# Replanning an instruction order: transfers at traced length, spare time for buffers, outputs and routing

## The chip, the cores and the metric

The kernel runs on one core of a Trainium2 chip. The metric is the device time of one execution in microseconds; the median of three executions is what is compared. The profile shows one execution in detail.

## The reference: what is computed

Three parts follow each other. A linear recurrence runs over 768 time steps for 4 x 8 heads, with a 40 x 40 state per head:

```
y[t]  = r[t] @ state
Sa    = state @ a[t]
state = state * w[t] - outer(Sa, b[t]) + outer(v[t], k[t])
```

Its output, 3072 tokens of 320 numbers, is routed: each token goes to the one of 8 experts with the largest gate logit, through a two-layer net with ReLU (320 to 1024 to 320), and is scaled by its gate probability. A last dense two-layer net (320 to 2048 to 320, leaky ReLU) follows for all tokens. Everything is in float32.

## The kernel before

The recurrence is done in chunks of 32 time steps. The 768 time steps are 6 blocks (`i`) of 4 chunks (`g`), and the heads come in two halves (`hf`), so that there are 48 steps `s = 8 i + 2 g + hf`. For each block and half (`n = 2 i + hf`) the inputs are loaded in two parts (`load(n, h)`: tiles `w`, `KB`, `AE`), decay products are formed on DVE and POOL (`prep`: L371 to L381), and inner products of the chunks on PE (`gram`: L409), which go to DRAM (`Md`). For a whole block they come back as `Mu`, a triangular system is solved in 14 rounds on DVE (`inverse`: L450, L452), the result goes to DRAM (`Td`, `Tad`) and back as `TB` and `Rt` (`back`), and `fix` completes it (PE L476, L485). Then for each step: `rv(s)` loads `RE` and `MV`, `kbt` transposes (L512), `chain` carries the state (PE L542, L553, L570, DVE L574), `output` forms the result (PE L590, L603, L622, DVE L611). After every fourth step of a half, `Router.add` computes the gate and scatters rows to `xs` with an indirect transfer from POOL (L870). Eight transfers `xs<-maskZ` of 563.5 KB (`zero_region`, L809) fill the regions of the experts beforehand. The two nets follow, with an order written out by hand, in which nothing is planned.

The order of all the work of the recurrence is made when the kernel is built, by a list scheduler, `Sched`. Each `op` has an engine (`V` DVE, `A` ACT, `P` POOL, `T` PE, `S` SyncE), a duration, tiles read and written, and for a transfer a length `xfer`. `run` computes for each operation a level (how early it must start so that what follows meets its due time, which `when(s)` sets to `START + STEP * s`) and then places the operations one after the other: on each engine among those that could start soonest, that with the highest level. `PATIENCE`, `SLACK` and `ALPHA` weigh the level against starting later. On the planned time line transfers share one bus, and at most eight are under way (`lanes`). Where PE's planned gap is over `GAP`, the plan fills a share of it (`FILL` 0.8, in the startup `FILL0` 0.685) with matmuls that compute nothing that is used (L724); they keep TensorE active. What comes out is only an order for each engine: at run time every engine goes through its list in that order, and each instruction waits for its data. The planned times do not bind.

All loads, the round trips over DRAM and the zero regions are issued by SyncE (SP) in one list, so a transfer whose buffer is still in use holds back all that stand behind it.

Of the kernel before, what the change touches and what calls it, by code (L numbers as in the profile page):

```python
# [26 lines left out]
class Sched:  # L27
# [7 lines left out]
    def __init__(self, eng):  # L35
        self.eng = dict(zip('VAPTS', eng))
        self.ops = []
        self.due = 1e9
        self.since = 0.
        self.slack = 0.  # L40
        self.w, self.r = {}, {}

    def op(self, on, dur, fn, r=(), w=(), ring=None, done=0., grp=None, xfer=0., banks=(), sel=False, act=None):

        i = len(self.ops)
        deps = set()
        for k in r:
            if k in self.w:
                deps.add(self.w[k])
        for k in w:  # L50
            if k in self.w:
                deps.add(self.w[k])
            deps.update(self.r.get(k, ()))
        deps.discard(i)
        for k in r:
            self.r.setdefault(k, set()).add(i)
        for k in w:
            self.w[k] = i
            self.r[k] = set()
        on = on if isinstance(on, dict) else {on: dur}  # L60
        self.ops.append(dict(on=on, fn=fn, deps=deps, ring=ring, done=done, grp=grp, users=0, ps=None, xfer=xfer, banks=list(banks), due=self.due, since=self.since, slack=self.slack, sel=sel, act=act))
        return i

    def psum(self, i, j):
# [18 lines left out]
    def run(self):  # L83
        ops = self.ops
        n = len(ops)
        succ = [[] for _ in ops]
        for i, o in enumerate(ops):
            for d in o['deps']:
                succ[d].append(i)
        lag = lambda o, e: self.AFTER[e] + o['done'] + (o['xfer'] + 1.5 if o['xfer'] else 0.)  # L90
        level = [0.] * n
        for i in range(n - 1, -1, -1):
            o = ops[i]
            e, d = min(o['on'].items(), key=lambda x: x[1])
            level[i] = d + max([level[j] + lag(o, e) for j in succ[i]] + [-o['due']])
        left = [len(o['deps']) for o in ops]
        at = [o['since'] for o in ops]
        free = {e: 0. for e in 'VAPTS'}
# [7 lines left out]
        grp = {}  # L106
# [13 lines left out]
        while placed < n:  # L120
            best = None
            for e in 'VAPTS':
                cand = []
                for i in wait[e]:
                    o = ops[i]
# [82 lines left out]
            seen = end + self.AFTER[e] + o['done']  # L208
            if o['xfer']:
                bus = max(bus, end + .65) + o['xfer']  # L210
                seen = bus + .95
                lanes = lanes[1:] + [seen]
            if o['done'] > 1.:
                scat = max(scat, seen)
            for j in succ[i]:
                left[j] -= 1
                at[j] = max(at[j], seen)
                if not left[j]:
                    offer(j)
        self.end = max(free.values())  # L220
# [8 lines left out]

    TICK, LEAST, COLD, FILL1 = 10.24 / 3, 3060., 1.85, 12.  # L230
    GAP, FILL, FILL0, FILLT = 0.24, 0.8, 0.685, 60.0
    SLACK, PATIENCE, ALPHA = 0.075, 30.677, 0.105


NV, QI, GS = 1, 'S', 0
SLACK0, LD0, LDS, PR0, PRS, LATEW, RV0, ZR0, ZRS, GR = 0.268, 0.0, 3.0, 15.245, 0, 0, 40.584, 52.618, 7.65, 1
NMV, NRE, NNI, NZ, NWT = 6, 7, 2, 3, 6


START, STEP = 66.553, 7.916  # L240
DPREP, DINV, DOUT, DTURN, DFIX = (-1.52, -1.13, -0.18, 1.52), (2.13, 2.32), 1.968, 0.886, 6.599
EVT = 'A'
EZ = 'AV'
PM, ZM = 0, 0
# [29 lines left out]
def attention(ctx, tc, I, R, eng):  # L274
# [62 lines left out]
    def masks(E):  # L337
# [2 lines left out]
            P.affine_select(maskP[o:o + 32], maskP[o:o + 32], [[1, 32]], ALU.is_gt, 0.0, base=0, channel_multiplier=-1)  # L340
        P.memset(maskZ, 0.0)
        P.iota(maskZ.bitcast(I32)[:, D:D + 1], [[0, 1]], base=NT, channel_multiplier=0)
    def dma(o, i, nb, r, w, on='S'):
        op(on, .48 if on == 'S' else .06, lambda E: E.dma_start(o, i), r, w, xfer=max(.18, nb / 360e3))  # L344

    def hold(i, fn):
        pass
# [1 line left out]
    def load(n, h):  # L349
        i, hf = divmod(n, 2)  # L350
        a = n % 4
        late = ['Mu'] if n in (2, 3) else []
        dma(ws[hf][:, h, 0:528], I['wT'][hf, i, :, 528 * h:528 * h + 528], 270336, late if LATEW else (), [('w', hf, h)])
        dma(KBs[a][:, 2 * h:2 * h + 2].rearrange("x g p a t -> x (g p a t)"), I['kbT'][hf, i, :, 1024 * h:1024 * h + 1024], 1 << 19, late, [('KB', a, h)])
        src = I['aT'][hf, i].rearrange("x (j g c) -> x j g c", j=2, g=4)[:, :, 2 * h:2 * h + 2]
        zero = [('AEs', a, j, g, par) for j in range(2) for g in (2 * h, 2 * h + 1) for par in range(2)]
        if i:
            dma(AEs[a][:, :, 2 * h:2 * h + 2].rearrange("x j g p t -> x j (g p t)"), src.rearrange("x j g c -> x j (g c)"), 1 << 19, late, [('AEo', a, j, h) for j in range(2)] + zero)
        else:
            for j in range(2):  # L360
                o, r = SIG[j], RHO[j]
                op('P', .45, lambda E, o=o, j=j: E.memset(AEs[a][o:o + 64, j, 2 * h:2 * h + 2], 0.0), (), zero[4 * j:4 * j + 4])
                dma(AEs[a][r:r + 64, j, 2 * h:2 * h + 2].rearrange("x g p t -> x (g p t)"), src[r:r + 64, j].rearrange("x g c -> x (g c)"), 1 << 17, late, [('AEo', a, j, h)])
# [71 lines left out]
    def when(s):  # L435
        Q.due = START + STEP * s
# [20 lines left out]
    def back(i):  # L457

        for gp in range(2):
            dma(TB4s[i % 2][:, gp].rearrange("s h u t -> s (h u) t"), Tds[i % 2][16 * gp:16 * gp + 16].rearrange("u q s t -> (q s) u t"), 262144,  # L460
                [('Td', i % 2)], [('TB', 4 * (i % 2) + 2 * gp + h) for h in range(2)], QI)
        for q in range(4):
            dma(R4[32 * q:32 * q + 16].rearrange("s m u t -> s (m u) t"), Tads[i % 2][:, q].rearrange("u s t -> s u t"), 80000, [('Tad', i % 2)], [('Rt', m, q) for m in range(4)], QI)
# [31 lines left out]
    def rv(s):  # L495
        i, g, hf, n = info(s)
        RE, MV = REs[s % NRE], MVs[s % NMV]
        dma(RE.rearrange("x j p t -> x (j p t)"), I['rT'][hf, i, :, 512 * g:512 * g + 512], 1 << 18, (), [('REo', s % NRE, j) for j in range(2)] + [('REs', s % NRE, j, par) for j in range(2) for par in range(2)])
        for j in range(2):
            r, o = RHO[j], SIG[j]  # L500
            dma(MV[o:o + 32, :, MC[j]], I['vt'][hf, i, j, :, 320 * g:320 * g + 320].rearrange("x (p e) -> x p e", e=40), 40960 * 4, (), [('MVv', s % NMV, j)])
            if s < 2:
                op('P', .35, lambda E, r=r, j=j: E.memset(MV[r:r + 40, :, MC[j]], 0.0), (), [('MVs', s % NMV, j)])

# [77 lines left out]
    def output(s):  # L582
# [41 lines left out]
        if g == 3:  # L624
            xk = []
            for bb in range(2):
                x = (2 * n + bb) % R.NXB
                xk.append(x)
                u = 8 * bb
                while u < 8 * bb + 8:  # L630
                    b, col = place(hf, u)
                    m = min(8 * bb + 8 - u, 12 - col // 40)
                    op('V', .15 + .0416 * m, lambda E, x=x, u=u, b=b, col=col, m=m, bb=bb:
                       E.tensor_tensor(R.xbs[x][:, 40 * (u - 8 * bb):40 * (u - 8 * bb) + 40 * m], py[:, b, col:col + 40 * m], Wts[n % NWT][:, u:u + m, :].rearrange("p h e -> p (h e)"), ALU.mult),
                       [('py', hf, k) for k in range(4)] + [('Wt', n % NWT, h, j) for h in range(2) for j in range(2)], [('xb', x, u)], banks=[('py', b)])
                    u += m
            R.add(Q, psum, copy, ev, hf, i, xk)


    Q.slack = SLACK0  # L640
# [48 lines left out]
    for i in range(6):  # L689
        if i < 5:  # L690
            for h in range(2):
                for n in (2 * i + 2, 2 * i + 3):
                    when(8 * i + DPREP[2 * h + n % 2])
                    load(n, h)
                    prep(n, h)
                    for g in (2 * h, 2 * h + 1):
                        gram(n, g)
            inverse(i + 1)
            when(8 * i + DFIX)
            back(i + 1)  # L700
            for x in range(4):
                when(8 * i + DFIX + .5 + x // 2 * 1.5)
                fix(i + 1, x % 2, x // 2)
            when(8 * i + DTURN)
            turn(2 * i + 2)
            turn(2 * i + 3)
        for c in range(8):
            s = 8 * i + c
            _, g, hf, n = info(s)
            when(s)  # L710
            Q.since = RV0 if 2 <= s < 8 else 0.
            rv(s)
            Q.since = 0.
            kbt(s)
            chain(s)
            if i == 0 and c < 4:
                Q.since = ZR0 + ZRS * c
                for e in (2 * c, 2 * c + 1):
                    R.zero_region(Q, e, maskZ, [('X', s % 2)])
                Q.since = 0.  # L720
            when(s + DOUT)
            output(s)
    Q.run()
    Q.emit(lambda: T.matmul(py[:, 2, 320:448], R.one, R.one, start=True, stop=True))  # L724
    R.finish(psum)
# [701 lines left out]
```

## Time and profile before

| what | value |
|---|---|
| time, median of 3 runs | 1150.17 us (1149.91 to 1153.44) |
| the profiled execution's own time | 1148.05 us |
| its span, first to last instruction | 1146.3 us |
| mean granted TensorE clock | 0.931 |
| PE busy | 1009.7 us, 88% |
| DVE, ACT, POOL busy | 735.6, 552.8, 378.5 us |
| time on the last chain: PE, DVE, issue, DMA, SP queue | 56%, 14%, 13%, 5%, 3% |

The first 545 us of the span are the recurrence with its routing, the rest are the two nets. A granted clock of 1.0 is 2.4 GHz and 0.5 is 1.2 GHz. "issue" is time in which an engine waited for nothing that the profile shows.

### The profile page before, as it was taken

What the parts mean: (1) busy time and instruction counts of PE and PEld (TensorE: products, weight loads), DVE (VectorE), ACT (ScalarE), POOL (GpSimd) and SP (SyncE); (2) the same over time, 40 slices, a digit from 0 to 9 for tenths busy, and PEclk for the clock granted to TensorE, in tenths of its full rate; (3) what the DMA queues carried; (4) which work ended last, traced back from release to release, by engine and by line L of the source; (5) the groups of instructions that cost most, each with busy time, mean ns of one, the idle gap of its engine ahead of it and who ended that gap; (6) DMA issues with size and microseconds to landing.
All of it is one profiled execution on the core that took longest, in us unless ns stands there. A gap on an engine that the chain in (4) does not pass through costs nothing.

```text
span 1146.3 us, 37065 instructions
## 1 busy us (share of the span) xinstructions
PE 1009.7 (88%) x15918; PEld 906.1 (79%) x15918; DVE 735.6 (64%) x1571; ACT 552.8 (48%) x1264; POOL 378.5 (33%) x318
## 2 busy tenths in 40 slices
PE   4677777888878879989589999999999999999997
PEld 4665667777767767778588888999989999999997
DVE  7984676976967856344577787786764444444453
ACT  4114554856746747667434434434533333333343
POOL 8232112222223221010155565662849191010100
PEclk9876888998989988889799999999999999999999
DMA  7659463653734723330565666753311010000000
GB/s 201 202 135 250 100 164 90 178 150 110 194 98 146 172 64 98 72 98 12 165 224 175 199 197 199 217 170 107 99 32 51 18 30 18 7 18 7 23 13 14
DMA packets 146123, 129.44 MB, mean 113 GB/s; under 512 B 102176, under 2 KB 110624, under 8 KB 145952
## 3 DMA queue, kind: packets, MB, share of 16 engines
q1 hardware_dynamic: 143648, 119.11, 37.7%
q0 software_dynamic: 2304, 7.89, 1.9%
q8 instruction: 127, 2.08, 0.8%
q14 instruction: 44, 0.36, 0.1%
HBM read 102.13 MB, written 24.85 MB: 111 GB/s over the span
## 4 chain that ended last, share of the span: by engine, by line
PE 56%; DVE 14%; issue 13%; ACT 6%; DMA 5%; POOL 3%; SPq 3%; POOLq 0%; DVEq 0%; ACTq 0%
PE ph L981 17%; PE py L622 4%; PE oy L1188 3%; PE oy L1187 3%; PE oy L1186 3%; PE ch L570 2%; PE tr L590 2%; SPq L344 2%; PE tr L409 2%; ACT Z L292 2%; PE tr L512 2%; DVE tmp L450 2%; ACT NI L292 2%; PE y L1046 2%; PE tr L485 2%
## 5 line engine op out<-in xcount | busy, mean ns | idle before, releaser
L981 PE MATMUL ph<-xt,wq 128*128 128x512 f32 (+2 forms) x1408 | 311.5, 364 | 5.0 <-DVE xt L1022 5.0
L981 PEld LDWEIGHTS ph<-xt,wq 128*128 128x128 f32 x1408 | 248.0, 189 | 35.5 <-DVE xt L1022 6.5
L1166 DVE TENSOR_TENSOR gf<-gf,ph 128x512 f32<-128x512 f32 (+1 forms) x112 | 68.4, 610 | 98.8 <-ACT gf L1165 98.4
L1170 DVE TENSOR_TENSOR gl<-gf,gh 128x512 fp32r<-128x512 f32 (+1 forms) x112 | 76.7, 684 | 70.1 <-ACT gh L1169 70.1
L1165 ACT ACTIVATE gf<-ph 128x512 f32<-128x512 f32 (+1 forms) x112 | 60.0, 536 | 109.5 <-PE ph L981 109.0
L292 ACT COPY Z<-tr 40x512 f32<-40x512 f32 x192 | 98.3, 540 | 22.9 <-PE tr L590 21.2
L1169 ACT CAST gh<-gf 128x512 fp32r<-128x512 f32 (+1 forms) x112 | 62.7, 559 | 96.3 <-DVE gf L1166 96.3
L381 POOL TENSOR_TENSOR KB<-KB,w 128x1024 f32<-128x1024 f32 x21 | 47.2, 2245 | 159.4 <-PE py L622 34.4
L1196 POOL DMA_INDIRECT out_dram<-ob,gid x24 | 23.9, 995 | 218.5 <-ACT ob L1195 213.3
L1032 ACT ACTIVATE gh<-ph 128x448 fp32r<-128x448 f32 x64 | 34.9, 546 | 120.3 <-PE ph L981 120.3
L1188 PE MATMUL oy<-wo,gl 128*128 128x320 f32 x288 | 89.2, 310 | 0.1
L1187 PE MATMUL oy<-wo,gh 128*128 128x320 f32 x288 | 88.9, 309 | 0.0
L1186 PE MATMUL oy<-wo,gh 128*128 128x320 f32 x288 | 88.8, 308 | 0.0
L622 PE MATMUL py<-Z,RE 128*32 128x40 f32 x1536 | 73.7, 212 | 6.1 <-DVE RE L611 4.6
L611 DVE TENSOR_TENSOR RE<-tr,maskP 64x128 f32<-64x128 f32 x192 | 55.1, 287 | 34.3 <-PE tr L603 30.4
L622 PEld LDWEIGHTS py<-Z,RE 128*32 128x32 f32 x1536 | 65.8, 120 | 13.6 <-DVE RE L611 7.5
L1046 PE MATMUL y<-gh,wo 128*128 128x448 f32 x192 | 73.1, 381 | 3.0 <-DVE Y L1053 2.8
L574 DVE TENSOR_TENSOR MV<-ch,WC 40x320 f32<-40x320 f32 x92 | 44.9, 488 | 45.3 <-PE ch L570 43.7
L870 POOL DMA_INDIRECT xs<-xb,rii x24 | 25.6, 1068 | 142.0 <-DVE rii L860 95.2
L1049 PE MATMUL y<-gl,wo 128*128 128x448 f32 x192 | 70.9, 369 | 0.0
L292 ACT COPY NI<-tr 64x160 f32<-64x160 f32 x192 | 55.1, 287 | 23.3 <-PE tr L512 20.0
L590 PE MATMUL tr<-ident,MV 128*104 128x128 f32 x384 | 60.2, 290 | 5.1 <-ACT NI L292 4.1
(173 smaller groups left out, 2206.2 us busy)
## 6 DMA issues: line engine op xcount, KB each, us to landing
KB<-in_kbT_dram SPq DMA_DIRECT2D x24, 512.0 KB, 6.0
RE<-in_rT_dram SPq DMA_DIRECT2D x48, 256.0 KB, 4.3
AE<-in_aT_dram SPq DMA_DIRECT2D x20, 512.0 KB, 6.3
raw<-in_wo_dram SPq DMA_DIRECT2D x16, 640.0 KB, 5.2
raw<-in_wqa_dram SPq DMA_DIRECT2D x16, 512.0 KB, 4.1
w<-in_wT_dram SPq DMA_DIRECT2D x24, 264.0 KB, 4.6
xs<-maskZ SPq DMA_DIRECT2D x8, 563.5 KB, 5.5
win<-xs SPq DMA_DIRECT2D x8, 563.5 KB, 10.0
```

Source lines behind the costliest of these rows:

```text
L292: (E.copy if E is A else E.tensor_copy)(o, i)
L590: E.transpose(c['t'][0:104, q, :], MV[:, 4 * h + q], ident)
L622: E.matmul(py[32 * g:32 * g + 32, b, col:col + 40], RE[:, j, p, :], Z[:, p, ZC[j]:ZC[j] + 40], start=True, stop=True)
L981: T.matmul(ph, l, r, start=k == 0, stop=k == 7)
L1046: T.matmul(y[c], hi, gh, start=m == 0, stop=False)
L1049: T.matmul(y[c], hi, gl, start=False, stop=m == 7)
L1166: V.tensor_tensor(gf, gf, ph, ALU.max)
L1169: A.copy(gh, gf)
L1170: V.tensor_tensor(gl, gf, gh.bitcast(F32), ALU.subtract)
L1186: T.matmul(o, gh[:, sl], w[:, 0:320], start=m == 0, stop=False)
L1187: T.matmul(o, gh[:, sl], w[:, 320:640], start=False, stop=False)
L1188: T.matmul(o, gl[:, sl], w[:, 0:320], start=False, stop=m == 15)
```

## The change

Only constants and rules of the planner change; the instructions themselves, their tiles and buffers stay. A transfer is planned with a bus rate of 230e3 bytes per us instead of 360e3, with 2.0 us instead of 0.95 us from its end to being seen, and with a further 0.816 us (`LATE`) for whoever reads it. A load marked `free=True` (w, KB, AE, RE, MV) is placed on the planned line no sooner than 4.829 us (`SPARE`) after the last user of its buffer, and that user becomes more urgent by as much. Each dependency of an output's operations has 0.065 us (`SPO`) of spare time, of routing and `fix` 0.296 us (`SPF`). `load` is due 0.127 steps ahead of its `prep`. The due times and weights have new values.

```diff
-    def op(self, on, dur, fn, r=(), w=(), ring=None, done=0., grp=None, xfer=0., banks=(), sel=False, act=None):
+    def op(self, on, dur, fn, r=(), w=(), ring=None, done=0., grp=None, xfer=0., banks=(), sel=False, act=None, free=False):
...
-        self.ops.append(dict(on=on, fn=fn, deps=deps, ring=ring, done=done, grp=grp, users=0, ps=None, xfer=xfer, banks=list(banks), due=self.due, since=self.since, slack=self.slack, sel=sel, act=act))
+        self.ops.append(dict(on=on, fn=fn, deps=deps, ring=ring, done=done, grp=grp, users=0, ps=None, xfer=xfer, banks=list(banks), due=self.due, since=self.since, slack=self.slack, sel=sel, act=act, spare=self.spare if on.keys() != {'S'} else self.SPARE if xfer and free else 0.))
...
-        lag = lambda o, e: self.AFTER[e] + o['done'] + (o['xfer'] + 1.5 if o['xfer'] else 0.)
+        lag = lambda o, e: self.AFTER[e] + o['done'] + (o['xfer'] + 2.2 if o['xfer'] else 0.)
...
-            level[i] = d + max([level[j] + lag(o, e) for j in succ[i]] + [-o['due']])
+            level[i] = d + max([level[j] + lag(o, e) + ops[j]['spare'] for j in succ[i]] + [-o['due']])
...
-                seen = bus + .95
+                seen = bus + 2.
...
-                at[j] = max(at[j], seen)
+                at[j] = max(at[j], seen + ops[j]['spare'] + (self.LATE if o['xfer'] else 0.))
...
-    SLACK, PATIENCE, ALPHA = 0.075, 30.677, 0.105
+    SPARE, LATE = 4.829, 0.816
+    SLACK, PATIENCE, ALPHA = 0.075, 47.288, 0.091
...
-SLACK0, LD0, LDS, PR0, PRS, LATEW, RV0, ZR0, ZRS, GR = 0.268, 0.0, 3.0, 15.245, 0, 0, 40.584, 52.618, 7.65, 1
+SLACK0, LD0, LDS, PR0, PRS, LATEW, RV0, ZR0, ZRS, GR = 0.338, 0.0, 3.0, 14.472, 0.072, 0, 40.584, 52.618, 7.65, 1
...
-START, STEP = 66.553, 7.916
-DPREP, DINV, DOUT, DTURN, DFIX = (-1.52, -1.13, -0.18, 1.52), (2.13, 2.32), 1.968, 0.886, 6.599
+LEAD, SPO, SPF = 0.127, 0.065, 0.296
+START, STEP = 72.1, 8.135
+DPREP, DINV, DOUT, DTURN, DFIX = (-1.52, -1.13, -0.18, 1.52), (2.28, 3.1), 1.966, 1.269, 7.992
...
-    def dma(o, i, nb, r, w, on='S'):
-        op(on, .48 if on == 'S' else .06, lambda E: E.dma_start(o, i), r, w, xfer=max(.18, nb / 360e3))
+    def dma(o, i, nb, r, w, on='S', free=False):
+        op(on, .48 if on == 'S' else .06, lambda E: E.dma_start(o, i), r, w, xfer=max(.18, nb / 230e3), free=free)
...
-            dma(TB4s[i % 2][:, gp].rearrange("s h u t -> s (h u) t"), Tds[i % 2][16 * gp:16 * gp + 16].rearrange("u q s t -> (q s) u t"), 262144,
+            dma(TB4s[i % 2][:, gp].rearrange("s h u t -> s (h u) t"), Tds[i % 2][16 * gp:16 * gp + 16].rearrange("u q s t -> (q s) u t"), 400000,
...
+            Q.spare = SPF
             R.add(Q, psum, copy, ev, hf, i, xk)
+            Q.spare = SPO
...
+                    when(8 * i + DPREP[2 * h + n % 2] - LEAD)
+                    load(n, h)
                     when(8 * i + DPREP[2 * h + n % 2])
-                    load(n, h)
                     prep(n, h)
...
+                Q.spare = SPF
                 fix(i + 1, x % 2, x // 2)
+                Q.spare = 0.
...
             when(s + DOUT)
+            Q.spare = SPO
             output(s)
+            Q.spare = 0.
```

## Rows read from the trace of the kernel before

**Rows 1.** Windows by stage, all engines; columns in the first row.
```profile
core 0: us, PE busy (x) PEld busy (x) DVE busy (x) ACT busy (x) POOL busy (x), PEclk, DMA share, GB/s
0.00:66.00 66.00, 37.47 (x595) 34.93 (x595) 57.54 (x110) 19.41 (x43) 37.23 (x69) 0.90 0.62 180
66.00:92.00 26.00, 19.80 (x504) 17.99 (x506) 16.60 (x35) 5.85 (x19) 6.12 (x3) 0.71 0.73 169
92.00:124.00 32.00, 20.15 (x602) 16.92 (x601) 16.02 (x31) 14.17 (x41) 5.82 (x4) 0.71 0.87 232
124.00:187.00 63.00, 52.70 (x1640) 45.57 (x1637) 49.04 (x137) 35.25 (x99) 12.54 (x8) 0.86 0.50 124
187.00:504.00 317.00, 267.32 (x8338) 232.75 (x8338) 218.26 (x662) 204.46 (x574) 71.46 (x65) 0.89 0.47 122
504.00:545.00 41.00, 39.09 (x1066) 33.62 (x1064) 18.83 (x64) 32.30 (x87) 2.31 (x6) 1.00 0.21 59
545.00:1146.30 601.30, 573.19 (x3204) 524.35 (x3193) 359.28 (x537) 241.32 (x402) 243.02 (x165) 0.98 0.31 94
```

**Rows 2.** Waits of PE, 187 to 545: total us, times, longest.
```profile
PE tr L485 <- issue: 9.7, 6, 2.3
...
PE tr L590 <- ACT NI L292: 3.8, 5, 1.0
...
PE py L724 <- issue: 0.3, 1, 0.3
...
PE tr L590 <- ACT MV L292: 0.2, 1, 0.2
```

**Rows 3.** DMA queues and issues of the whole span: count, KB, us to landing.
```profile
q8 instruction: 127, 2.08, 0.8%
...
KB<-in_kbT_dram SPq DMA_DIRECT2D x24, 512.0 KB, 6.0
...
xs<-maskZ SPq DMA_DIRECT2D x8, 563.5 KB, 5.5
```

**Rows 4.** DMA view, whole span, same columns.
```profile
TB<-Td SPq DMA_DIRECT2D x12, 256.0 KB, 4.4
```

**Rows 5.** SP timeline, 66 to 170: start us, us, issue.
```profile
67.37 0.34 SPq L344 DMA_DIRECT2D Td<-Tt  x1
...
71.52 1.33 SPq L809 DMA_DIRECT2D xs<-maskZ  x2
72.89 1.55 SPq L344 DMA_DIRECT2D TB<-Td  x1
74.48 5.67 SPq L344 DMA_DIRECT2D Rt<-Tad  x4
```

**Rows 6.** SP timeline, 170 to 330, the same transfers one block later.
```profile
216.07 0.34 SPq L344 DMA_DIRECT2D Td<-Tt  x1
...
219.65 0.40 SPq L344 DMA_DIRECT2D TB<-Td  x1
220.14 3.68 SPq L344 DMA_DIRECT2D Rt<-Tad  x4
```

**Rows 7.** Chain that ended last, 66 to 100: start us, us, what.
```profile
79.67 2.21 DMA Rt<-Tad
...
92.00 4.75 DMA w<-in_wT_dram
...
96.77 1.26 DVE W L371
```

**Rows 8.** Waits of PE, 66 to 124: total us, times, longest.
```profile
PE ch L553 <- issue: 7.8, 2, 5.6
...
PE tr L409 <- issue: 0.4, 2, 0.2
```

**Rows 9.** PE lines, 187 to 545, the filling matmuls: busy, mean ns.
```profile
L724 PE MATMUL py<-one 128*128 128x128 bf16 x215 | 20.1, 235 | 0.9 <-DVE xb L634 0.6 <-issue 0.3
```

**Rows 10.** SP queue waits, 0 to 500: total us, times, longest.
```profile
SPq L344 <- PE tr L590: 91.0, 29, 12.5
```

More of the change, by code (lines that the diff above doesn't have):

```diff
@@ L40, in __init__ @@
         self.slack = 0.
+        self.spare = 0.
         self.w, self.r = {}, {}
-    def op(self, on, dur, fn, r=(), w=(), ring=None, done=0., grp=None, xfer=0., banks=(), sel=False, act=None):
+    def op(self, on, dur, fn, r=(), w=(), ring=None, done=0., grp=None, xfer=0., banks=(), sel=False, act=None, free=False):
         i = len(self.ops)
@@ L352, in load @@
         late = ['Mu'] if n in (2, 3) else []
-        dma(ws[hf][:, h, 0:528], I['wT'][hf, i, :, 528 * h:528 * h + 528], 270336, late if LATEW else (), [('w', hf, h)])
-        dma(KBs[a][:, 2 * h:2 * h + 2].rearrange("x g p a t -> x (g p a t)"), I['kbT'][hf, i, :, 1024 * h:1024 * h + 1024], 1 << 19, late, [('KB', a, h)])
+        dma(ws[hf][:, h, 0:528], I['wT'][hf, i, :, 528 * h:528 * h + 528], 270336, late if LATEW else (), [('w', hf, h)], free=True)
+        dma(KBs[a][:, 2 * h:2 * h + 2].rearrange("x g p a t -> x (g p a t)"), I['kbT'][hf, i, :, 1024 * h:1024 * h + 1024], 1 << 19, late, [('KB', a, h)], free=True)
         src = I['aT'][hf, i].rearrange("x (j g c) -> x j g c", j=2, g=4)[:, :, 2 * h:2 * h + 2]
@@ L357, in load @@
         if i:
-            dma(AEs[a][:, :, 2 * h:2 * h + 2].rearrange("x j g p t -> x j (g p t)"), src.rearrange("x j g c -> x j (g c)"), 1 << 19, late, [('AEo', a, j, h) for j in range(2)] + zero)
+            dma(AEs[a][:, :, 2 * h:2 * h + 2].rearrange("x j g p t -> x j (g p t)"), src.rearrange("x j g c -> x j (g c)"), 1 << 19, late, [('AEo', a, j, h) for j in range(2)] + zero, free=True)
         else:
@@ L497, in rv @@
         RE, MV = REs[s % NRE], MVs[s % NMV]
-        dma(RE.rearrange("x j p t -> x (j p t)"), I['rT'][hf, i, :, 512 * g:512 * g + 512], 1 << 18, (), [('REo', s % NRE, j) for j in range(2)] + [('REs', s % NRE, j, par) for j in range(2) for par in range(2)])
+        dma(RE.rearrange("x j p t -> x (j p t)"), I['rT'][hf, i, :, 512 * g:512 * g + 512], 1 << 18, (), [('REo', s % NRE, j) for j in range(2)] + [('REs', s % NRE, j, par) for j in range(2) for par in range(2)], free=True)
         for j in range(2):
             r, o = RHO[j], SIG[j]
-            dma(MV[o:o + 32, :, MC[j]], I['vt'][hf, i, j, :, 320 * g:320 * g + 320].rearrange("x (p e) -> x p e", e=40), 40960 * 4, (), [('MVv', s % NMV, j)])
+            dma(MV[o:o + 32, :, MC[j]], I['vt'][hf, i, j, :, 320 * g:320 * g + 320].rearrange("x (p e) -> x p e", e=40), 40960 * 4, (), [('MVv', s % NMV, j)], free=True)
             if s < 2:
```

## The prediction, made before the change was run

> **What bounds the kernel now.** I read the windows first, cut into stages, then PE's waits, the chain of waits in the startup, and last the SP queue, because the change acts through the order in which SP issues.
>
> The table of windows [rows 1] gives five stages of the recurrence. Up to 66 us DVE is the engine that is full: 57.5 of 66 us. From 66 to 92 and from 92 to 124 none is full; PE is busy for 19.8 of 26 and 20.2 of 32 us, and the share of the DMA engines rises to 0.73 and 0.87. From 124 on PE leads: 52.7 of 63 us, then 267.3 of 317, then 39.1 of 41. The granted clock is 0.71 from 66 to 124 and 0.89 from 187 to 504, so part of each stage runs at 1.2 GHz, the lower level. Behind 545 us stands 601.3 us of the two nets, 52% of the span, whose order is not planned and which I leave as it is.
>
> Two things hold PE up. From 187 to 545 its waits [rows 2] are ten rows with the releaser "issue", 9.7 us for the first and 0.3 for the last, 39.2 us in all, and ten rows with data as releaser, 3.8 us for the first and 0.2 for the last, 10.8 us in all; no row there names a DMA. So after the first block SP's order is not what PE waits for. The "issue" waits stand in front of the densest groups, and PE's instructions are themselves brought by DMA: the instruction queue moved 127 packets with 2.08 MB [rows 3], about 16.4 KB each.
>
> In the startup it is otherwise. The triangular solution is written at 67.37 (Td), but its way back (TB) is issued only at 72.89, behind four small writes and two zero regions issued at 71.52; the four Rt transfers take SP from 74.48 to 80.15 [rows 5]. The chain of waits goes through all of it, ends with a Rt that lands at 81.88, and later goes through a load of w issued at 92.00 that takes 4.75 us, on which DVE's scan (1.26 us) depends [rows 7].
>
> **The planner's error.** With the old constants a KB load is 0.65 + 524288/360e3 + 0.95 = 3.06 us on the plan; traced are 6.0 [rows 3]. TB is 0.65 + 0.73 + 0.95 = 2.33, traced 4.4 [rows 4]. The new constants, LATE included, give 5.75 for KB and 5.21 for TB. A zero region keeps its 1.6 us on the bus, goes from 3.2 to 5.07, and is traced at 5.5 [rows 3]. So the plan comes near what the chip does, most of all where the bus is full, which the stage from 92 to 124 is.
>
> **The change part by part.** No instruction is removed or added but the filling matmuls, whose number comes out of the plan.
>
> A, the way of Td and back. From the Td issue to the last of the four Rt issues took 80.15 - 67.37 = 12.8 us. One block later, without zero regions in between, it took 220.14 + 3.68 - 216.07 = 7.75 us [rows 5, 6]. The difference, 5.0 us, is what a clean order is worth. A bus seen as full and a longer path behind Td both raise TB and Rt above the zero regions, which nothing needs until the first scatter. Bounds 0 and 5.0; I take 4.0, because the four small writes may stay in front. Behind this gain stands PE, which then starts `fix` earlier; DVE is idle there (16.6 of 26 us), so nothing takes the gain at once.
>
> B, the load of w at 92.00. It was queued behind `RE`, `MV` and zero regions, and the scan that waits for it stands on DVE in front of the state's multiplication. With `load` due 0.127 steps earlier and its length known, the scan would not stand in the way. Bounds 0 and the scan itself, 1.26 us; I take 1.2, since the chain does pass there.
>
> C, PE's "issue" waits in the startup. From 66 to 124 they are four rows, 7.8 us for the first and 0.4 for the last, 12.2 us together [rows 8], while 39.2 us over 358 us later make 6.4 us for 58. The excess of 5.8 us falls where DMA is fullest. If loads and zero regions are spread further, part of it goes. Bounds: a loss of the same 5.8 and a gain of it; I take 2.5, not half of it, since the bytes to be moved are the same. The Trainium skill (Runtime: NRT & Kernel Launch, section "Instruction fetch mechanics") says that instructions are refilled in blocks of 16 KiB and that this is mostly hidden. The block size agrees with the 16.4 KB per packet here; the 39.2 us of "issue" do not agree with "mostly hidden". By that rule C would be 0 and the forecast 2.5 us later.
>
> D, spare time for outputs, routing and `fix`. It acts on PE's data waits, 10.8 us from 187 to 545 [rows 2], of which ACT's NI copies make 3.8 in front of L590. With 0.065 us more on each dependency the plan puts other work of PE between producer and user. Bounds 0 and 10.8; I take 2.0, because a wait of around 1 us is long against 0.065 us, and the spare time only reorders where other work is ready. In routing and `fix` (0.296 us) the waits are mostly "issue", which spare time doesn't touch.
>
> E, the 4.829 us of spare time for load buffers. It moves loads back in SP's list, so SP stands less often before a buffer in use: for L590 alone it stood 91.0 us in 29 waits [rows 10]. Yet no chain of PE's waits after 187 goes through SP, so I count 0. What hides it is the distance between a load and its use; if that cover is gone, a load is late by up to 4.829 + 0.816 = 5.6 us, which is a rival below. The due times, PATIENCE and ALPHA reorder everything a little: no row prices that, I count 0 and let the range carry it. From A and C the clock may rise as well: not counted.
>
> Sum: 4.0 + 1.2 + 2.5 + 2.0 = 9.7 us. The profiled execution took 1148.05 us, so 1138.4 in its own terms. It is 2.1 us below the median of 1150.17; against the median the forecast is 1140.5 us.
>
> **The rivals.** *PE keeps its pace (no change).* PE's order is as dense as before, "issue" waits only move, and a startup that is 5 us shorter is given back before 545 because the first blocks run into the same instruction waits. Speaking for it: 39.2 of 50 us of PE's waits are of a kind the plan doesn't know [rows 2]. Against it: the startup's waits are visibly SP's [rows 5, 7]. Time: 1147 to 1153.
>
> *More filling matmuls (slower).* START goes from 66.553 to 72.1 and STEP from 7.916 to 8.135. If these follow the plan's own length, it is longer by 5.5 + 48 x 0.219 = 16 us, while PE's work is the same; the additional time is gaps on PE, and 0.8 of it, 12.8 us, becomes filling matmuls. These are instructions in PE's list: where the data is there in time they are pure delay. From 187 to 545 there are now 215 of them, 20.1 us busy [rows 9]. They would take the place of D's waits: 1150.2 - 7.7 + 12.8 = 1155 us. It decides from about 8 us of additional filling on, that is 28 us in place of 20.1. Against it: due times are only weights, and a longer plan may lie all in the startup, where PE waits anyway.
>
> *Late loads (slower).* If a planned load lands 5.6 us later than its user once per block, and the next block's `inverse` stands behind it, one to two blocks give 6 to 11 us, less the startup's gain: 1152 to 1154, or more when every block has it. It decides where the distance from a load's landing to its user is under 5.6 us. For it speaks that DVE's scan already waited for a w load [rows 7]; against it that no DMA row is among PE's waits after 187. The Trainium skill (DMA: Bandwidth & Descriptors, section "Rules for kernel authors") advises to issue a transfer early and to wait late, which by its letter speaks against spare time in front of loads.
>
> *A calm queue helps everywhere (much faster).* If spread transfers take the "issue" waits down by a third in all blocks as well, 13 us of 39.2 go on top: 1127 us. For it: DMA share 0.47 on the mean from 187 to 504 hides full stretches. Against it: the waits stand before the densest groups of small matmuls, which stay.
>
> **How the numbers follow.** Forecast, 1134 to 1146: 0.45. Much faster, 1122 to 1134: 0.15. No change, 1147 to 1153: 0.15. Filling matmuls: 0.17; late loads: 0.06; slower by the mere reordering, around 1156: 0.02. A change of 0.3%, 3.45 us, is what this kernel's measurement can tell from none. So faster 0.60, same 0.15, slower 0.25. The range leaves out the far half of the much faster case and the far part of the slower ones: 1126 to 1157. The likeliest case alone has 1134 to 1146.
>
> **What the profile after will show.** Right: TB and Rt follow Td within about 8 us and the zero regions come behind them (A); no scan waits for w near the first outputs (B); "issue" waits of PE from 66 to 124 near 9 us (C); PE's data waits from 187 on near 9 us (D); the filling matmuls near 215 in the later blocks; the recurrence ends near 535. Wrong: filling matmuls over 28 us, DMA rows among PE's waits after 187, or a startup as long as before. What would overturn it most easily is PE's pace from 187 to 504, where 1% is 3.2 us, a third of the forecast.

## The result, and the profile after

The changed kernel is slower: 1166.46 us median (1161.73 to 1171.43, 4 runs) against 1150.53 us (1149.91 to 1153.44, 4 runs), ratio 1.0141 with a 95% interval of 1.0101 to 1.0181. The forecast was 1140.5 us. The time lies outside the range of 1126 to 1157 us, on the slow side. The profiled execution took 1171.43 us, the slowest of the four; its span is 1169.7 us.

The windows by stage of the changed kernel, columns as in [rows 1]:

```profile
66.00:92.00 26.00, 25.52 (x437) 24.75 (x438) 13.32 (x36) 4.70 (x16) 7.21 (x4) 0.89 0.60 151
92.00:124.00 32.00, 18.82 (x694) 16.50 (x693) 9.15 (x21) 10.33 (x32) 3.61 (x3) 0.66 0.82 222
...
187.00:504.00 317.00, 273.40 (x8198) 237.38 (x8199) 217.33 (x647) 194.37 (x551) 75.59 (x64) 0.88 0.50 126
```

The matmuls of the recurrence's last output now end at 562.4 us, where they ended at 542.4 before; of the 23.4 us by which the span grew 20.0 lie there and 3.4 behind it. From 66 to 92 PE is busy for 25.5 of 26 us, and yet no output comes earlier. What PE does there shows in its timeline (start us, us, line, operation, count, idle time before it):

```profile
79.11 9.50 PE L735 MATMUL py<-one 128*128 128x128 bf16 x167
88.54 1.62 PE L413 MATMUL tr<-AE,KB 128*64 128x64 f32 x48
...
91.60 2.35 PE L735 MATMUL py<-one 128*128 128x128 bf16 x39
93.88 1.45 PE L480 MATMUL tr<-Rt,TB 16*32 16x16 f32 x128
```

L735 are the filling matmuls (L724 before), L413 the inner products, L480 the first `fix`. It comes at 93.88 us, where the last wait for Rt in the kernel before ended at 81.88 [rows 7]. The grouped lines of PE give the fills: from 66 to 124 in the kernel before and in the changed kernel, then from 187 to 563 in the changed kernel:

```profile
L724 PE MATMUL py<-one 128*128 128x128 bf16 x98 | 8.1, 253 | 0.0
```
```profile
L735 PE MATMUL py<-one 128*128 128x128 bf16 x330 | 21.0, 227 | 0.0
```
```profile
L735 PE MATMUL py<-one 128*128 128x128 bf16 x367 | 30.6, 229 | 3.0 <-DVE xb L638 1.8 <-issue 1.2
```

The last answers to the 215 fills and 20.1 us of [rows 9]; over the whole program there are 1192 in place of 715. SP's timeline shows the way of Td and back:

```profile
64.12 0.33 SPq L348 DMA_DIRECT2D Td<-Tt  x1
...
67.62 0.92 SPq L820 DMA_DIRECT2D xs<-maskZ  x1
75.43 5.97 SPq L348 DMA_DIRECT2D Md<-mab  x8
81.44 0.45 SPq L348 DMA_DIRECT2D TB<-Td  x1
81.94 3.58 SPq L348 DMA_DIRECT2D Rt<-Tad  x4
```

Td is written 3.3 us earlier than in [rows 5], but TB is issued 17.3 us behind it instead of 5.5: four loads, a zero region and eight small writes stand between, and the small writes wait for inner products of PE. The first step's output group (L626) starts at 124.76 us, 16.7 us later than the 108.10 us of the kernel before. From there to the end of the last output it takes 437.6 us, before 434.3.

Where the 20.0 us lie shows in the stretch from the start to the end of the last output, in the kernel before and in the changed kernel:

```profile
0.00:542.40 542.40, 434.18 (x12651) 379.95 (x12652) 373.95 (x1022) 310.39 (x859) 135.47 (x153) 0.88 0.51 134
```
```profile
0.00:562.40 562.40, 460.49 (x13090) 405.67 (x13091) 371.90 (x1024) 308.78 (x858) 141.87 (x156) 0.87 0.50 129
```

PE is busy for 26.3 us more. The fills in it take 80.4 us, before 53.4; the rest is 380 us in both. PE waits 6.3 us less in all: its "issue" waits fell from 68.4 to 51.9 us, its waits for data rose from 38.0 to 48.7. So in this account the loss is 27.0 us of fills, less the waits in whose place some of them stand.

Some of the transfers became quicker. From the DMA view (KB each, us to landing), against 6.0 and 5.5 in [rows 3] and 4.4 in [rows 4]:

```profile
KB<-in_kbT_dram SPq DMA_DIRECT2D x24, 512.0 KB, 4.2
...
xs<-maskZ SPq DMA_DIRECT2D x8, 563.5 KB, 4.4
...
TB<-Td SPq DMA_DIRECT2D x12, 256.0 KB, 5.1
```

The loads of KB and the zero regions land sooner, TB later, and the loads of w and RE are as before (4.6 and 4.3 us). For a KB load the plan was too short before (3.06 us against 6.0) and is now too long (5.75 against 4.2).

### The profile page after: what moved, and what is told of

It reads as the page before. It is cut to its first block, busy times and chain, and to the rows that moved or that the text cites. A ratio compares the mean times of both kernels' runs of the same rounds, so it can differ in the third digit from the quotient of the medians.

```text
span 1169.7 us, 37997 instructions
## 1 busy us (share of the span) xinstructions
PE 1039.0 (89%) x16395; PEld 935.3 (80%) x16395; DVE 731.8 (63%) x1570; ACT 550.2 (47%) x1262; POOL 382.1 (33%) x321
## 4 chain that ended last, share of the span: by engine, by line
issue 23%; PE 22%; POOL 11%; DVE 7%; DMA 5%; ACT 3%; SPq 1%; POOLq 0%; DVEq 0%; ACTq 0%
PE ph L992 3%; PE py L626 3%; POOL gu L1220 3%; PE tr L594 2%; POOL fl L1223 2%; POOL gu L1221 2%; DVE wq L958 2%; DMA wa<-cvm 1%; POOL gu L1222 1%; PE ch L574 1%; POOL out_dram L1207 1%; PE py L735 1%; PE y L1057 1%; PE y L1060 1%; PE tr L607 1%
## 5 line engine op out<-in xcount | busy, mean ns | idle before, releaser
L296 ACT COPY Z<-tr 40x512 f32<-40x512 f32 (+1 forms) x192 | 97.3, 539 | 31.0 <-PE tr L594 29.4
L735 PE MATMUL py<-one 128*128 128x128 bf16 x1192 | 85.5, 230 | 4.6 <-DVE xb L638 2.9
L626 PE MATMUL py<-Z,RE 128*32 128x40 f32 x1536 | 74.9, 214 | 10.2 <-DVE RE L615 4.3
L735 PEld LDWEIGHTS <-one 128*128 128x128 bf16 x1192 | 75.5, 104 | 8.2 <-issue 5.4
L626 PEld LDWEIGHTS py<-Z,RE 128*32 128x32 f32 x1536 | 67.2, 122 | 16.0 <-DVE RE L615 6.8
L385 POOL TENSOR_TENSOR KB<-KB,w 128x1024 f32<-128x1024 f32 x22 | 51.5, 2340 | 86.9 <-DMA KB<-in_kbT_dram 43.1
```

What stands on the lines that cost most here:

```text
L296: (E.copy if E is A else E.tensor_copy)(o, i)
L626: E.matmul(py[32 * g:32 * g + 32, b, col:col + 40], RE[:, j, p, :], Z[:, p, ZC[j]:ZC[j] + 40], start=True, stop=True)
```

## The experiments

All ratios are to the kernel before on the same chip, with 95% intervals. The kernel before had medians from 1142.4 to 1150.5 us in the six comparisons, and its single executions mostly lay between 1134.6 and 1155.4, so that differences under half a per cent are mostly not settled.

**First: the fills, SP's order, the transfer lengths.** Two kernels change only how many fills are emitted:

```diff
-            for _ in range(self.fill.get(i, 0)):
+            for _ in range(int(.6 * self.fill.get(i, 0))):      # the changed kernel
+            for _ in range(int(1.667 * self.fill.get(i, 0))):   # the kernel before
```

> The changed kernel's order, instruction for instruction, but of the filling matmuls that the plan puts in only 0.6 are emitted (rounded down for each place): about 700 instead of 1192, as many as the kernel before has. Theory of the fills: the changed kernel loses its time to 477 more fills (85.5 us busy against 54.9), so 15 to 25 us come back, ratio to the kernel before 0.995 to 1.002. Theory of the startup's SP order (TB issued at 81.4 us instead of 72.9): the fills only stand where PE waits anyway, so the ratio stays 1.010 to 1.018. Theory of the granted clock: fewer fills lower the clock and it gets slower, over 1.018.

> The kernel before with its own order, but 1.667 times the filling matmuls at each place: about 1180 instead of 715, as many as the changed kernel has. Theory of the fills: slower by 15 to 25 us, ratio 1.013 to 1.022. Theory of the startup's SP order, or of another order in general: within 0.4% of the kernel before, since most fills stand where PE would wait.

The changed kernel with 693 fills: 1156.06 us, ratio 1.0126 (1.0063 to 1.0189). The kernel before with 1169: 1152.02 us, ratio 1.0109 (1.0045 to 1.0173). Both ratios are uncertain beyond their intervals: the kernel before had its lowest median here (1142.4 us, in the other five comparisons 1146.5 to 1150.5, once on the same chip). By the ratio alone the changed kernel with fewer fills stays in the interval of the change. By its own times it is quicker: its four executions (1154.9 to 1158.7 us) lie below all eight of the changed kernel in other comparisons (1161.7 and more). Its first output came at 109.9 us, 15 us earlier, and its last one ended at 548.6, 13.8 us earlier:

```profile
0.00:548.60 548.60, 439.34 (x12622) 380.98 (x12623) 372.94 (x1024) 308.71 (x858) 140.51 (x156) 0.86 0.50 132
```

With 28.8 us fewer fills (51.6 us), PE's waits for data rose from 48.7 to 64.0 us, and its other work took 387.7 us instead of 380, at a granted clock of 0.86 instead of 0.87. So fewer fills bring back a part of the loss, about half, and not all, because some of them stood where PE would have waited. Whether more fills cost the order before anything is not settled: 1152.0 us is 0.1 to 0.5% above its medians in the other comparisons.

The third moves six entries of SP's list, once the plan is made (`ways` and `puts` hold the numbers that these transfers got when they were planned):

```diff
     Q.run()
+    moved = [x for x in Q.order if x[1] in ways[0]]      # TB, Rt of block 0
+    Q.order = [x for x in Q.order if x[1] not in ways[0]]
+    k = [x[1] for x in Q.order].index(puts[0]) + 1       # behind Tad
+    Q.order[k:k] = moved
```

> The changed kernel with one thing moved: the six transfers that bring the first block's solution back (two TB, four Rt) are issued right behind the two that write it (Td, Tad), before the four loads, the zero region and the eight small writes that stand between them in the changed kernel. Theory of the startup's SP order: the first fix on PE comes 5 to 12 us earlier than 93.9 us and the end follows it by at least half, ratio 1.003 to 1.010. Theory of the fills: fix stands behind filling matmuls in PE's list and cannot start before them, so below 3 us come back. Theory that later blocks set the end: fix comes earlier, but the end stays within 3 us.

Ratio 1.0227 (1.0156 to 1.0298). SP issues TB 15 us earlier, and the first `fix` comes only 1 us earlier, as the fills in front of it are still in PE's list. SP's timeline, then PE's, of this kernel:

```profile
66.30 0.38 SPq L348 DMA_DIRECT2D TB<-Td  x1
```
```profile
78.08 9.50 PE L741 MATMUL py<-one 128*128 128x128 bf16 x167
...
92.84 1.31 PE L482 MATMUL tr<-Rt,TB 16*32 16x16 f32 x128
```

SP's order alone is not what holds the changed kernel's startup. The fourth has the transfer lengths of the change alone (`nb / 230e3`, `bus + 2.`, lag 2.2, LATE 0.816, TB as 400000):

> The kernel before with the transfer lengths of the change alone (bus rate 230e3, 2.0 us to being seen, lag 2.2, LATE 0.816, TB as 400000 bytes); due times, weights and spare times as before. Theory that longer planned transfers make the plan worse (PE gaps in the plan get filled, transfers are spread): as slow as the changed kernel or slower, ratio 1.010 to 1.03. Theory that the due times and weights did it: no slower than 1.004.

Ratio 1.0334 (1.0264 to 1.0405): alone they cost more than the whole change, even if the comparison's low median makes up half a per cent of it.

**Second: the parts of the change.** The changed kernel again, the change without its transfer lengths, and its spare times or its due times and weights alone on the kernel before:

```diff
-    START, STEP = 66.553, 7.916                # x8, with DINV, DOUT, DTURN, DFIX,
+    START, STEP = 72.1, 8.135                  # PATIENCE, ALPHA, SLACK0, PR0, PRS of the change
```

> The changed kernel itself, beside the next three on the same chip, since the two calls so far may have been on different ones: a ratio of 1.010 to 1.018 to the kernel before if the loss does not depend on the chip. In its profile the first fix on PE near 94 us, the first output near 125 us.

> The changed kernel with the planned transfer lengths of before (bus rate 360e3, 0.95 us to being seen, lag 1.5, LATE 0, TB as 262144 bytes); due times, weights and all spare times as in the change. Theory that longer planned transfers are the loss (alone they cost 3.3%): 15 us or more come back, ratio 1.000 or below, with the first fix near 82 us and fewer filling matmuls. Theory that the due times and spare times carry a loss of their own: the ratio stays above 1.008.

> The kernel before with only the spare times of the change (4.829 us for load buffers, 0.065 for outputs, 0.296 for routing and fix, loads due 0.127 steps earlier); transfer lengths, due times and weights as before. Theory that the transfer lengths are the loss: within 0.5% of the kernel before, or faster. Theory that any spare time lengthens the plan, and each lengthening is paid on the chip: slower, 1.005 to 1.02.

> The kernel before with only the due times and weights of the change (START, STEP, DINV, DOUT, DTURN, DFIX, PATIENCE, ALPHA, SLACK0, PR0, PRS). Theory that fix, due 1.4 steps later, is pushed into the block boundaries where the state's chain waits for it: slower, 1.005 to 1.015, with longer gaps between the last output of a block and the first of the next. Theory that the transfer lengths are the whole loss: within 0.5%.

The changed kernel: 1.0180 (1.0072 to 1.0288). Without its transfer lengths: 1.0259 (1.0177 to 1.0342). Spare times alone: 1.0193 (1.0109 to 1.0276). Due times and weights alone: 1.0237 (1.0158 to 1.0316). Each part alone costs about as much as all together or more, so the costs don't add up, and the theory that the transfer lengths are the loss falls: without them it is no faster. Nor is it the startup throughout: with the due times alone the first output comes at 99.5 us, 8.6 us before that of the kernel before, and the time is lost behind it. The windows from first to last output, of the kernel before, the changed kernel and that one:

```profile
108.10:542.40 434.30, 366.14 (x11241) 318.33 (x11239) 292.00 (x860) 276.44 (x772) 91.90 (x81) 0.89 0.46 120
```
```profile
124.80:562.40 437.60, 381.05 (x11365) 330.70 (x11364) 292.08 (x862) 273.54 (x768) 92.30 (x79) 0.88 0.46 115
```
```profile
99.50:567.70 468.20, 396.70 (x11400) 343.17 (x11390) 295.85 (x865) 277.50 (x776) 91.50 (x81) 0.85 0.44 115
```

The same steps take 34 us longer in the third, at a granted clock of 0.85 instead of 0.89.

**Third: the startup of the changed kernel.** Fills are taken out by their planned time `t`, with or without the move of TB and Rt; for fewer fills in everything behind the startup, 0.6 of those with `t > 95` are kept:

```diff
     Q.run()
+    for t, k, e in Q.order:
+        if 55 < t < 90:          # 50 to 70 in the kernel before
+            Q.fill.pop(k, None)
```

> The changed kernel, without the six runs of filling matmuls (325 of 1192) that stand in PE's list between the first block's inner products and its first fix, and with TB and Rt of the first block issued right behind Td and Tad. Theory that the startup is the whole loss (first output 16.7 us later than in the kernel before, the same 436 us from there to the last output): first fix near 76 us in place of 93.9, first output near 108, ratio 0.995 to 1.003. Theory that the blocks behind set the end and a later start is absorbed: the first output is as early, but the ratio stays at 1.008 or more, with a longer stretch from first to last output.

> The changed kernel without the same six runs of filling matmuls, SP's order untouched. Theory that PE's list holds fix back (TB issued 15 us earlier alone moved it by 1 us only): first fix at about 84 to 86 us, where TB lands, first output near 112, and 8 to 12 us come back, ratio 1.003 to 1.009. If instead the fills only stand in waits, the ratio stays 1.012 or more.

> The changed kernel with its startup untouched, and only 0.6 of the filling matmuls in everything planned behind it. Theory of the startup: no change to the changed kernel, ratio 1.012 to 1.02. Theory that later fills cost PE time: up to 12 us come back, ratio 1.004 to 1.010.

> The kernel before with the same two things done to its startup: no filling matmuls from the second half of the first block's inner products to fix (164 of 715), and TB and Rt right behind Td and Tad. If the way of Td and back sets the start, the first fix comes at 76 us in place of 81.9 and the first output 5 us earlier, ratio 0.993 to 0.998; if the clock that the fills keep up is worth more, or the blocks behind set the end, 0.999 to 1.006.

Startup without fills and TB and Rt moved: 1.0100 (1.0066 to 1.0134). The startup's fills alone: 1.0111 (1.0040 to 1.0181). Fewer later fills: 1.0169 (1.0087 to 1.0251). The kernel before with both: 0.9997 (0.9964 to 1.0031). With the startup's fills alone gone `fix` begins at 83.65 us instead of 93.88, the first output comes at 109.1 us, as early as in the kernel before, and the last one ends at 562.9, as late as in the changed kernel: 453.8 us in between. The window of that stretch:

```profile
109.10:562.90 453.80, 389.67 (x11365) 338.36 (x11364) 294.60 (x862) 274.61 (x768) 96.09 (x80) 0.86 0.45 115
```

This trace is of the slowest of four executions (1170.3 us, median 1164.95), so it shows more loss behind the startup than the others had. The kernel before with both has its first output 3.9 us earlier and takes the same time. So a part of an earlier start is absorbed by the blocks behind, and the intervals don't tell how much comes back; it is no rule, since with fewer fills everywhere (the first experiment) the equally early start was kept to the end. With both, the first `fix` came at 86.95 us and the first output only at 119.1, since PE's "issue" waits between them came to 15.4 us, against 6.5 with the startup's fills alone gone. The longest is 6.95 us:

```profile
116.80 0.47 PE L548 MATMUL ch<-MV,AE 128*32 128x40 f32 x11 [6.95 <-issue]
```

**Fourth: other orders with nothing of the change.** Three kernels move one or a few constants of the kernel before a little; a fourth takes back one due time inside the change; a fifth moves four constants inside it; a sixth adds the move of TB and Rt to the first. The diff shows two of them:

```diff
-    SLACK, PATIENCE, ALPHA = 0.075, 30.677, 0.105
+    SLACK, PATIENCE, ALPHA = 0.075, 23.23, 0.105     # z1, and w2 with the move of TB and Rt
-START, STEP = 66.553, 7.916
+START, STEP = 66.553, 8.01                           # z2
```

> The kernel before with PATIENCE 23.23 in place of 30.677, nothing of the change: another order from the startup on, 730 filling matmuls in place of 715. Theory that each part of the change does harm of its own: within 0.5% of the kernel before. Theory that the constants before are a tuned point and any other order is slower: 1.008 to 1.025.

> The kernel before with STEP 8.01 in place of 7.916 (the change goes to 8.135), nothing else: another order from the startup on, 791 filling matmuls. Theory of harm by the parts themselves: within 0.7%. Theory of the tuned point: 1.008 to 1.025.

> The kernel before with SLACK 0.085 for 0.075, PATIENCE 32.8 for 30.7, SLACK0 0.283 for 0.268 and DFIX 6.315 for 6.599 (fix due earlier, the other way than in the change): an order that differs as much as those of the change's parts, 999 filling matmuls. Theory of harm by the parts: no more than 1.008, since nothing of the change is in it. Theory of the tuned point: 1.015 to 1.035, as much as the parts of the change.

> The changed kernel with fix due as early as before (DFIX 6.599 in place of 7.992), the rest of the change kept. Theory that fix, pushed to the block boundaries, is the loss: the gaps between a block's last output and the next block's first shrink from about 29 to 23 us, ratio 1.005 or less. Theory of the tuned point: the change's constants fit each other, and moving one alone makes it slower still, 1.02 or more.

> The changed kernel with ALPHA 0.098 for 0.091, STEP 8.169 for 8.135, DINV (2.144, 2.797) for (2.28, 3.1) and DFIX 7.871 for 7.992: the same transfer lengths and spare times, another order, 1072 filling matmuls in place of 1192, so fewer planned gaps on PE. Theory that the constants of the change fit its lengths badly: ratio 1.008 or less to the kernel before. Theory that planning with these lengths and spare times is slower whatever the constants: 1.010 to 1.025, as the changed kernel.

> The kernel before with PATIENCE 23.23 (which alone gave 0.9915) and with TB and Rt of the first block issued right behind Td and Tad. Theory that the startup counts: 0.985 to 0.990. Theory that an earlier first output is absorbed by the blocks behind: 0.989 to 0.995, no different from PATIENCE alone.

The table has the orders that the planner gave, the unchanged emission only, with the number of fills in the trace:

| order | fills | ratio to the kernel before |
|---|---|---|
| before, PATIENCE 23.23 (z1) | 730 | 0.9915 (0.9880 to 0.9950) |
| before | 715 | 1 |
| before, STEP 8.01 (z2) | 791 | 1.0088 (1.0054 to 1.0122) |
| before, due times of the change (x8) | 856 | 1.0237 (1.0158 to 1.0316) |
| before, spare times of the change (x7) | 925 | 1.0193 (1.0109 to 1.0276) |
| change without its transfer lengths (x6) | 979 | 1.0259 (1.0177 to 1.0342) |
| before, SLACK 0.085 and three more (z3) | 999 | 1.0223 (1.0182 to 1.0265) |
| before, transfer lengths of the change (x4) | 1030 | 1.0334 (1.0264 to 1.0405) |
| change, DFIX as before (z4) | 1041 | 1.0267 (1.0222 to 1.0311) |
| change, four constants moved (w1) | 1072 | 1.0185 (1.0091 to 1.0280) |
| change | 1192 | 1.0141 (1.0101 to 1.0181) |

Orders without anything of the change reach from 0.9915 to 1.0223. The theory that only the change's own parts do harm falls, by z3, whether or not they do some as well; that the kernel before is the best point falls too, by z1. The same kind of small move inside the change (w1, z4) gives 1.0185 and 1.0267. That `fix` is due later in the change is no cause: due earlier it is slower, though the gap from the start of a block's last output to that of the next block's first did shrink, from 28, 30, 31, 29 and 20 us to 26, 29, 27, 24 and 16. PATIENCE 23.23 with TB and Rt moved (w2) has 0.9961 (0.9920 to 1.0001); it does not differ clearly from PATIENCE alone. PATIENCE alone, 1138.9 us against 1147.94 on the same chip, is the version that beats both kernels, in one comparison.

What z3 loses shows in its window from first to last output: 458.1 us, PE busy 383.4 of it, so 74.7 us of waits where the kernel before has 68.2; the rest is fills, 39.6 us in place of 22.7. x8 instead runs at a lower clock, and the changed kernel has more fills and fewer waits than the kernel before. The losses have no single form.

## Why the prediction was wrong

The step that failed stands under E: "The due times, PATIENCE and ALPHA reorder everything a little: no row prices that, I count 0 and let the range carry it." That term is larger than all the others together. The due times and weights of the change alone, on the kernel before, took 1176.95 us against 1148.74, 28 us more; A to D together were 9.7 us. With nothing of the change, moved constants give from 9 us less to 25 us more (1138.9 and 1172.7 against 1147.9). The parts from which A to D were to gain cost time by themselves as well (transfer lengths 1.0334, spare times 1.0193). Each of A to D was worked out as if the rest of the order stayed, which it doesn't.

A had the wrong sign. I let the longer planned transfers raise TB and Rt above the rest. In the new plan four loads, a zero region and eight small writes came first, TB was issued 17.3 us behind Td, and from 66 to 124 us PE's list held 330 fills in place of 98, most of them in front of `fix`. Even with TB issued at once, `fix` moved by 1 us; without the fills it began 10.2 us earlier. What I had not seen is that a longer plan also writes fills into PE's list, and at run time those are executed whether the data is there or not.

B was right in its small way: no scan waits for a load of w near the first outputs, the scan now stands behind the state's multiplication. It gave nothing, because that multiplication itself came later (at 112.09 us, before at 98.06). C did not come: PE's "issue" waits from 66 to 124 are four rows, 13.5 us in place of 12.2 [rows 8], though DMA's share fell from 0.87 to 0.82 from 92 to 124. From 187 to the recurrence's end they fell from 39.2 to 33.3 us, which no step of mine had. The rule of the Trainium skill (Runtime: NRT & Kernel Launch, section Instruction fetch mechanics) that stands there, by which C is 0, came nearer here than my 2.5 us; that the cost is mostly hidden does not agree with the 33.3 us. D failed: PE's waits for data from 187 on are 12.4 us, before 10.8. (The windows up to 545 us are six, where I counted five stages; nothing hangs on it.)

Of the rivals, that of the filling matmuls was nearest: it named 28 us of fills from 187 on as the point where it decides, there are 30.6, and it gave 1155 us. Its mechanism holds in part: fills lengthen the startup (fills away, first output 15.7 us earlier), and in the account of the recurrence they are 27.0 us more. But in the changed kernel neither fewer fills everywhere (1.0126, about half of the loss by its own times) nor fewer in one part (1.0111, 1.0169) takes the loss away, so they are not shown to be the whole cause. Late loads: no DMA row is among PE's waits from 187 on, so that didn't happen.

Shown is: the change's parts don't add, an order made without any of them is as slow, and the first output's time does not decide the end (99.5 us in one of the slow orders, 124.8 in the changed kernel). Argued, from single traces, is that the fills are about half of the changed kernel's loss. Open is what makes one order's blocks slower than another's: fills, clock and waits all differ between the orders, with no one row that follows the time.

## What to carry to other kernels

A planner that writes an order for engines that work in order is not improved term by term: a truer cost gives another order, and another order by itself was worth up to 2% here. Before a change to such a planner is credited or blamed, time a few orders that differ by small moves of its constants; that spread is the smallest effect that can be told. And work that a plan puts into a gap (filling matmuls) should be looked at as an instruction in front of the next one: when the plan's gap is too long, it delays. Taken away, it gives back only what the next instruction doesn't spend waiting.

## What the runs showed of the hardware that was not expected

PE stood for up to 6.95 us inside a group of equal small matmuls, with no data to wait for. The records of single DMA packets in the traces tell what such waits are. In the kernel before 27 of the 28 "issue" waits of at least 0.8 us between 66 us and the last output, and in the changed kernel all 22, ended 1.1 to 1.7 us after a 16 KiB packet of the instruction queue did; of the waits for data that long only 1 of 10 and 1 of 5 did, about what chance gives. So PE waits there for its next instructions. In the case of 6.95 us the packet started only 4.7 us after PE had stopped, while the DMA engines were busy for 0.97 of the wait; that the data transfers held it up is likely, not shown. Taking away the fills in front of a dense group did not shorten these waits much: from 66 to 124 us they are 12.2 us without the startup's fills and 13.5 us with them.

The granted clock over the recurrence went from 0.89 to 0.85 by order alone (due times of the change on the kernel before); there PE was busy for 396.7 us in place of 366.1, of which fills make 31.0 and 22.7 us, so nearly the same work took 22 us more. One and the same program varied by 1.3% between executions (1134.6 to 1149.8 us within one comparison), far more than the three first times of the kernel before let expect.
